# Seven products in place of eight for half of the first matrix product, in fp16, and three elementwise steps moved to GpSimd

## The chip, the cores and the metric

The kernel runs on one core of a Trainium2 chip. A core has five engines, each with a queue of its own that works in order: TensorE (matmuls, in the profile PE, with its weight loads PEld), VectorE (DVE), ScalarE (ACT), GpSimd (POOL) and SyncE (SP, which here only issues DMAs). Matmuls write to PSUM, which has eight banks of 512 fp32 values for each of 128 partitions; VectorE and ScalarE read and write it, GpSimd does not here. SBUF is the working memory. The metric is the time of one execution in microseconds (us), the median of several runs.

## The reference

Linear attention with phi(x) = elu(x) + 1, then a two-layer network with GELU on its output, for 8 batches of 8 heads, 576 rows and 64 values:

```python
def phi(x):
    return np.where(x > 0, x, np.exp(x) - 1.0) + 1.0
q_p, k_p = (phi(q), phi(k))
kv = np.einsum('bhsd,bhse->bhde', k_p, v)
z = np.sum(k_p, axis=2)
num = np.einsum('bhsd,bhde->bhse', q_p, kv)
den = np.einsum('bhsd,bhd->bhs', q_p, z)[..., None] + 1e-06
attn_out = num / den                                      # (8, 8, 576, 64)
x = attn_out.transpose(0, 2, 1, 3).reshape(B * S, H * D)  # 4608 x 512
h = x @ w_in                                              # w_in 512 x 2048
g = 0.5 * h * (1.0 + np.tanh(c * (h + 0.044715 * h * h * h)))
out = g @ w_out                                           # w_out 2048 x 512
```

Inputs and output are fp32.

## The kernel before

The 4608 rows of x are cut into nine groups. Groups 0 to 7 are the first 512 rows of each batch; group 8 gathers the last 64 rows of all eight. `iteration(j)` does group j's network, and beside it the attention of group j+1 and the preparation of later batches. Every engine issues in the order in which the Python code emits its instructions (`manual_schedule`), so the order is written by hand: a group's matmuls are a list of steps, and `at(j, slot, fn)` hangs other work behind step number `slot` of group j.

A group from 2 on has 16 steps for h and 7 for the output. A step `("h", m)` is four matmuls (`h_mm`, L394: 128 columns of `w_in_sb` as weights, 512 columns of the transposed x `xt` moving, both bf16, summed over d_model in one PSUM bank) and one GELU on ScalarE (`gelu`, L409) that writes block m of `g` in fp16. Its blocks are taken in the order 0, 8, 1, 9, ... The output of the group is then computed by Strassen's scheme in Winograd's form with seven products instead of eight (`Products`): g and w_out are each cut into two by two quarters, VectorE makes sums of quarters of g (`sums`, `third_sum`, `last_sum`, L763; those of w_out are made once, L752), each product is 16 matmuls of 256 columns (L790), and ScalarE and VectorE combine the results out of PSUM into `o_sb` (L834, L821, L862). Products come in the order 1, 5, 6, 7, 2, 4, 3.

The tiles of one PSUM pool share six banks ("b"), and a new tile takes the bank that came free first; the pair of banks "a" serves attention alone.

Attention of batch b is done in group b-1: after step 9 (group 2: 12) `nab_quads` issues 32 matmuls of q with the k-v products into four banks and the pair (L332), then 72 for the k-v product of batch b+1 (`kv_paired`, L254). At once VectorE divides (`divide`, L287 and L288) into `xs`, and SyncE issues four DMA transposes of `xs` into `xt` (L694). k and q go through `exp_of` (ScalarE), `linear_of` (max(x+1, 1), VectorE, L230) and `least_of` (their minimum, VectorE, L238); v is cast to bf16 by VectorE (L243); q is transposed by DMA (`least_q`, L671). For batches 5 to 7 this is `plan_prepare`: q's linear part and the v cast at the start of a group, k's linear part behind step 10, exponentials behind steps 15 and 16, minima behind 17 and 20. The loads of k, q and v (L94, L103) and of q's last rows (`load_rest`, L117; mapped in `plan_rest`) are issued by SyncE into a pool of seven buffers, `pld`. The output is stored by DMAs on ScalarE's queue (L875).

Of the kernel before, what the change touches and what calls it, by code (L numbers as in the profile page):

```python
# [8 lines left out]
FP32 = mybir.dt.float32  # L9
# [7 lines left out]
def kernel(  # L17
# [20 lines left out]
    P = 128  # L38
# [20 lines left out]
    pout = ctx.enter_context(tc.tile_pool(name="pout", bufs=2))  # L59
    psm = ctx.enter_context(tc.tile_pool(name="psm", bufs=2))  # L60
    pkv = ctx.enter_context(tc.tile_pool(name="pkv", bufs=1))
    ps_b = ctx.enter_context(
        tc.tile_pool(name="ps_b", bufs=6, space=bass.MemoryType.PSUM)
    )
# [6 lines left out]


    ident = const.tile([P, P + 64], BF16, name="ident")[:, 0:P]
    w_in_sb = const.tile([P, KM, d_ff], BF16, name="w_in_sb")
    w_out_sb = const.tile([P, 2, MM, N2], FP16, name="w_out_sb")
    w_sum = const.tile([P, 3, MM // 2, N2], FP16, name="w_sum")

    def bank(name, shape, dt=FP32):
        return ps_b.tile(shape, dt, name=name, tag="b")
# [98 lines left out]

    warm = const.tile([P, 512], BF16, name="warm")
    nc.vector.memset(warm, 0.0)  # L182
    make_identity(nc, ident)
    vps = [pkv.tile([P, J * NP, E], BF16, name=f"vp{i}") for i in range(2)]
    kvbds = [pkv.tile([P, NP, 2 * E], BF16, name=f"kvbd{b}") for b in range(3)]
    kvs = {b: pkv.tile([P, NP, E], BF16, name=f"kv{b}") for b in range(3, B)}
    for i in range(2):
        nc.gpsimd.memset(vps[i][:, :, D:E], 1.0)
# [32 lines left out]
            o, i = o[..., cs, :], i[..., cs, :]  # L221
        nc.scalar.activation(o, i, AF.Exp)  # L222

    def linear_of(name, b, hs=None):
        x = ld[name, b]
        hs = hs or slice(0, x.shape[1])
        if (name, b) not in phi:
            phi_tiles(name, b)
        o, i = maps_view(name, b, x, phi[name, b], hs)
        nc.vector.tensor_scalar(o, i, 1.0, 1.0, op0=ALU.add, op1=ALU.max)  # L230

    def least_of(name, b, hs=None, cs=None):
        p, e = phi[name, b], exps[name, b]
# [62 lines left out]

    def x_tile(b, c):
        if b not in xs:
            xs[b] = pxs.tile([P, C, d_model], BF16, name="xs")
        return xs[b][:, c]  # L300

    def by_parity(x):
# [12 lines left out]
            divide(by_parity(x)[:, a], ns[a].rearrange("p (u e) -> p u e", e=E))  # L315
        return x

    def nab_quads(qt_cs, bs, kv_b):

        ns = [[bank("n_ps", [P, 6 * E]) for _ in range(2)] for _ in range(2)]
        n_pair = pair_of_banks("n_ps")
        ns.append([n_pair[:, s] for s in range(2)])
        units = [(c, i, a) for c in range(C) for i in range(2) for a in range(2)]
        for n, (c, i, a) in enumerate(units):
            g = n // 6
            one = bs[c][0] == bs[c][1]
            for t in range(1 if one else 2):
                for s in range(2):  # L330
                    cs = slice(0, P) if one else slice(HP * t, HP * (t + 1))
                    nc.tensor.matmul(  # L332
                        ns[g][s][cs, E * (n - 6 * g) : E * (n - 6 * g + 1)],
                        lhsT=qt_cs[c][HP * s : HP * (s + 1), 2 * a + i, cs],
                        rhs=kv_of_head(bs[c][t], s, 2 * a + i),
                        skip_group_check=True,
                    )
        if kv_b is not None:
            for ii in range(2):
                kv_paired(kv_b, ii, lambda a, ii: n_pair[:, a, E * (4 + ii) : E * (5 + ii)])  # L340

        def x_of(transposed):
            x = pxs.tile([P, C, d_model], BF16, name="xs")
            x_v = x.rearrange("p c (i s a d) -> p s (c i) a d", s=2, a=2, d=D)
            for g in range(2):
                for s in range(2):
                    divide(
                        x_v[:, s, 3 * g : 3 * (g + 1)],
                        ns[g][s].rearrange("p (k a e) -> p k a e", a=2, e=E),
                    )  # L350
                for c in ((0,), (1, 2))[g]:
                    transposed(c, x[:, c])
            n_v = n_pair[:, :, 0 : 4 * E].rearrange("p s (k a e) -> p s k a e", a=2, e=E)
            divide(x_v[:, :, 6:8], n_v)
            transposed(3, x[:, 3])
            if kv_b is not None:
                nc.vector.tensor_copy(
                    out=kvs[kv_b].rearrange("p (a i) e -> p a i e", a=2),
                    in_=n_pair[:, :, 4 * E : 6 * E].rearrange("p a (i e) -> p a i e", e=E),
                )  # L360

        return x_of
# [19 lines left out]
        )  # L382

    def transpose_x(x, xt_c, fn, blocks=range(NP)):
        t_ps = bank("t_ps", [P, len(blocks), P], BF16)
        for n, i in enumerate(blocks):
            nc.tensor.transpose(t_ps[:, n, :], x[:, P * i : P * (i + 1)], ident)  # L387
        fn(out=xt_c[:, blocks.start : blocks.stop], in_=t_ps)

    xts, qts = {}, {}  # L390
# [35 lines left out]
    def first_batch():  # L426
# [44 lines left out]
        for i in range(2):  # L471
            cast_w_out(i, nc.gpsimd.tensor_copy)

        xts[0] = pt.tile([P, NP, MAIN], BF16, name="xt")
        x = {0: x_tile(0, 0)}

        def t(c, blocks=range(NP)):
# [34 lines left out]

    fill = {}

    def at(j, slot, fn, *args):


        fill.setdefault((j, slot), []).append((fn, args))  # L520
# [5 lines left out]
    def plan_second():  # L526
# [43 lines left out]

        def t(c):
            if c == 0:
                xts[b] = pt.tile([P, NP, MAIN], BF16, name="xt")
            transpose_x(x[c], xt_chunk(b, c), nc.scalar.copy)

        at(0, 15, maps)
# [38 lines left out]
    def plan_fourth():  # L615

        for slot, hs in zip((9, 13), halves):
            at(1, slot, linear_of, "k", 3, hs)
        at(1, 17, exp_of, "k", 3)
        at(1, 18, exp_of, "q", 3)  # L620
        at(1, 18, exp_of, "k", 4)
        at(1, 18, gelu_table)
        at(1, 20, least_of, "k", 3)
        at(1, 21, linear_of, "q", 3)
        at(2, 0, cast_v, 3)
        at(2, 0, least_q, 3)
        at(2, 4, kv_in_pair, 3)
        at(2, 5, linear_of, "k", 4)
        at(2, 5, least_of, "k", 4)
        at(2, 5, cast_v, 4)  # L630
        at(2, 8, linear_of, "q", 4)
        at(2, 15, exp_of, "q", 4)
        at(2, 16, exp_of, "k", 5)
        at(2, 19, least_q, 4)
        at(2, 22, linear_of, "k", 5)
        at(3, 0, least_of, "k", 5)

    def plan_prepare(j):

        b = j + 2  # L640
        has_k = b + 1 < B
        at(j, 0, linear_of, "q", b)
        at(j, 0, cast_v, b)
        at(j, 15, exp_of, "q", b)
        at(j, 17, least_q, b)
        if has_k:
            at(j, 10, linear_of, "k", b + 1)
            at(j, 16, exp_of, "k", b + 1)
            at(j, 20, least_of, "k", b + 1)

    def plan_rest(m):
        j = 5 + m // 2

        def least():
            least_of("qr", m)
            if m == 0:
                qts[B] = pt.tile([P, C, NP, P], BF16, name="qt")
            nc.sync.dma_start_transpose(
                out=qts[B][:, m], in_=phi["qr", m][:, 0].rearrange("p h d -> p (h d)")
            )  # L660

        at(j, 6 if j == 5 else 0, linear_of, "qr", m)
        at(j, 15, exp_of, "qr", m)
        at(j, 18, least)

# [24 lines left out]

    def transposed_x(b, c, x):
        if b not in xts:
            xts[b] = pt.tile([P, NP, MAIN], BF16, name="xt")
        nc.sync.dma_start_transpose(out=xt_chunk(b, c), in_=x)  # L694

    def plan_attention(b):


        def attention():
            bs = [(b, b) if b < B else (2 * c, 2 * c + 1) for c in range(C)]  # L700
            x_of = nab_quads([qts[b][:, c] for c in range(C)], bs, b + 1 if b + 1 < B else None)
            x_of(lambda c, x: transposed_x(b, c, x))

        at(b - 1, 12 if b == 3 else 9, attention)

    def evac(dst, src, on_scalar):
        (nc.scalar.copy if on_scalar else nc.vector.tensor_copy)(dst, src)
# [48 lines left out]
    class Products:  # L756
# [113 lines left out]
        def store(self, h, o_sb, fs=slice(0, d_model)):  # L870
# [5 lines left out]
            else:  # L876
                for t in range(2):
                    self.store_rest(2 * h + t, o_sb[:, t], fs)

    def iteration(j):  # L880
        xt = xts[j]
        if j < B:
            g = pg.tile([P, 2, MM, MAIN // 2], FP16, name="g")
        else:
            g = pg.tile([P, MM, 2, MAIN // 2], FP16, name="g").rearrange("p m a n -> p a m n")
        hs = [("h", m) for m in range(MM)]
        us = [range(m, m + 4) for m in range(0, MM, 4)]
        products = Products(j, g) if j else None
# [4 lines left out]
        elif j == 1:  # L893
# [6 lines left out]
            at(1, 14, products.sums, early)  # L900
            at(1, 17, products.sums, late)
            at(1, 19, products.last_sum)
        else:
            steps = [hs[i + n] for i in range(MM // 2) for n in (0, MM // 2)]
            steps += [("product", n) for n in (1, 5, 6, 7, 2, 4, 3)]
# [2 lines left out]
                at(j, slot, products.third_sum, ms)  # L908
            at(j, 16, products.last_sum)
        o_pss = {}  # L910
        for slot, step in enumerate(steps):
            if step[0] == "h":
                m = step[1]
                h_ps = h_begun.get(j, {}).get(m)
                if h_ps is None:
                    h_ps = bank("h_ps", [P, MAIN])
                    h_mm(h_ps, xt, m)
                gelu(j, g, m, h_ps)
            elif step[0] == "product":
                products.step(step[1])  # L920
            else:
# [3 lines left out]
                o_mm(o_pss[t], g, t, u, half=(j, slot - 0.5))  # L925
                if u.stop == MM:
                    finish(j, t, o_pss[t])
            run(j, slot)

    plan_second()  # L930
    plan_third()
# [15 lines left out]
        at(5, 1, load_rest, m + 2)  # L947
    for j in range(2, 7):
        at(j, 16, gelu_table)

    for j in range(B + 1):
        iteration(j)
# [30 lines left out]
```

## Time and profile before

| | |
|---|---|
| time, median of 3 runs (lowest to highest) | 271.81 us (271.79 to 272.06) |
| span of the profiled execution, first to last instruction | 270.2 us; the page gives no other time of that execution |
| TensorE's granted clock | 0.999 |
| busy: TensorE, its weight loads | 264.4 us, 170.8 us |
| busy: VectorE, ScalarE, GpSimd | 164.7 us, 166.0 us, 15.0 us |
| first matmul for h of groups 3 to 8 | 104.66, 132.11, 159.56, 187.01, 213.76, 240.60 us |

In a profile L394 is line 394 of the kernel; a row names engine, line, operation, and output<-inputs with their shapes. In brackets stands how long the engine had been idle before the instruction and who ended that. Matmuls overlap, so a row's own length is more than its pitch; the pitch is read from the starts or from the chain of work that ended last, which is followed back from the last instruction.

### The profile page before, as it was taken

The page shows a single profiled execution, that of the slowest core. Times are in us where ns is not written, and L with a number is a line of the kernel's source. Part 1 is how long each engine was busy: PE and PEld are TensorE (multiplying, and loading weights), DVE is VectorE, ACT ScalarE, POOL GpSimd, SP SyncE. Part 2 cuts the span into 40 slices and gives each one's busy share as a digit, 9 for nine tenths or more (in the row PEclk, how much of TensorE's full clock was granted, in tenths as well). Part 3 has the DMA queues.
Part 4 walks back from the last instruction along what each step waited for, and adds up shares of the span by engine and source line. Part 5 has one row for each costly group of instructions (what it writes and reads, how often), then busy time and mean ns, then how long its engine had stood idle before and what let it go on. Part 6 is the DMA issues. An engine that isn't in the chain of part 4 may idle for free.

```text
span 270.2 us, 5941 instructions
## 1 busy us (share of the span) xinstructions
PE 264.4 (98%) x2533; PEld 170.8 (63%) x2533; DVE 164.7 (61%) x265; ACT 166.0 (61%) x225; POOL 15.0 (6%) x21
## 2 busy tenths in 40 slices
PE   8999999999999999999999999999999999999994
PEld 2584456465854686558655874587458745874584
DVE  2860186988999966788738774693267326622262
ACT  4768877799776683668266926582665265028700
POOL 3056401000000000000000000000000000000000
PEclk9999999999999999999999999999999999999999
DMA  6999999995799998893699474219231412121004
GB/s 234 401 405 396 410 408 400 400 382 98 232 290 257 327 245 222 292 295 78 172 355 268 91 151 137 61 39 159 96 41 43 135 56 61 19 113 45 0 2 155
DMA packets 59786, 53.87 MB, mean 199 GB/s; under 512 B 35696, under 2 KB 45936, under 8 KB 59760
## 3 DMA queue, kind: packets, MB, share of 16 engines
q1 hardware_dynamic: 56880, 44.57, 58.4%
q10 hardware_dynamic: 2880, 8.91, 8.7%
q8 instruction: 20, 0.33, 0.5%
q14 instruction: 6, 0.05, 0.0%
HBM read 36.70 MB, written 9.44 MB: 171 GB/s over the span
## 4 chain that ended last, share of the span: by engine, by line
PE 92%; DMA 3%; DVE 2%; SPq 1%; issue 0%; ACT 0%
PE h_ps L394 45%; PE o_ps L790 36%; PE o_ps L734 5%; DMA v_x<-in_v_dram 3%; PE n_ps L332 1%; PE kv_ps L254 1%; PE n_ps L254 1%; PE n_ps L270 1%; PE t_ps L387 1%; SPq L94 1%; DVE s L763 0%; SPq L99 0%; PE t_ps L545 0%; DVE kvbd L686 0%; DVE vp L243 0%
## 5 line engine op out<-in xcount | busy, mean ns | idle before, releaser
L394 PE MATMUL h_ps<-xt,w_in_sb 128*128 128x512 bf16 (+1 forms) x628 | 128.4, 361 | 0.2 <-issue 0.2
L409 ACT ACTIVATE g<-h_ps 128x512 f16<-128x512 f32 x144 | 86.8, 616 | 59.5 <-PE h_ps L394 57.5
L394 PEld LDWEIGHTS <-w_in_sb 128*128 128x128 bf16 x628 | 58.2, 98 | 62.4
L790 PEld LDWEIGHTS <-g 128*128 128x128 f16 x624 | 60.9, 98 | 9.0 <-ACT g L409 0.2
L790 PE MATMUL o_ps<-w_out_sb,g 128*128 128x256 f16 x496 | 58.2, 273 | 0.0
L862 DVE TENSOR_TENSOR o_sb<-o_ps,o_sb 128x512 f32<-128x512 f32 (+1 forms) x42 | 27.9, 665 | 29.4 <-PE o_ps L790 28.5
L763 DVE TENSOR_TENSOR s<-g 128x1024 f16<-128x1024 f16 x18 | 12.4, 691 | 40.0 <-ACT g L409 39.9
L790 PE MATMUL o_ps<-w_sum,s 128*128 128x256 f16 x256 | 29.3, 273 | 0.0
L790 PEld LDWEIGHTS <-s 128*128 128x128 f16 x272 | 26.6, 98 | 3.1
L288 DVE TENSOR_TENSOR xs<-n_ps,r 128x384 bf16<-128x384 f32 (+2 forms) x44 | 25.6, 582 | 1.5
L222 ACT ACTIVATE k_e<-k_x 128x2304 bf16<-128x2304 f32 (+1 forms) x9 | 17.2, 1910 | 3.7 <-DVE k_p L238 2.9
L834 ACT COPY o_sb<-o_ps 128x512 f32<-128x512 f32 x8 | 4.7, 583 | 22.3 <-PE o_ps L790 22.3
L230 DVE TENSOR_SCALAR q_p<-q_x 128x2048 bf16<-128x2048 f32 (+1 forms) x9 | 9.9, 1101 | 13.2 <-DMA q_x<-in_q_dram 13.2
L222 ACT ACTIVATE q_e<-q_x 128x2048 bf16<-128x2048 f32 (+1 forms) x10 | 15.7, 1568 | 2.9 <-DMA q_x<-in_q_dram 2.9
L790 PE MATMUL o_ps<-w_sum,g 128*128 128x256 f16 x128 | 15.3, 273 | 0.0
L734 PE MATMUL o_ps<-w_out_sb,g 128*128 128x512 f16 x64 | 15.1, 379 | 0.0
L230 DVE TENSOR_SCALAR k_p<-k_x 128x2304 bf16<-128x2304 f32 (+1 forms) x10 | 11.1, 1113 | 4.2 <-DMA k_x<-in_k_dram 4.1
L422 ACT ACT_TABLE_LOAD x9 | 11.5, 1283 | 0.2
L431 PE MATMUL w_ps<-warm 128*128 128x512 bf16 x32 | 10.3, 484 | 1.2 <-DVE warm L182 1.2
L763 DVE TENSOR_TENSOR s<-s,g 128x1024 f16<-128x1024 f16 x16 | 11.1, 692 | 0.5
L238 DVE TENSOR_TENSOR k_p<-k_p,k_e 128x2304 bf16<-128x2304 bf16 (+1 forms) x9 | 11.0, 1221 | 0.7 <-ACT k_e L222 0.3
L243 DVE CAST vp<-v_x 128x2304 bf16<-128x2304 f32 (+1 forms) x9 | 11.0, 1225 | 0.5 <-DMA v_x<-in_v_dram 0.4
(63 smaller groups left out, 151.3 us busy)
## 6 DMA issues: line engine op xcount, KB each, us to landing
out_dram<-o_sb ACTq DMA_DIRECT2D x16, 512.0 KB, 3.9
k_x<-in_k_dram SPq DMA_DIRECT2D x7, 1152.0 KB, 9.3
v_x<-in_v_dram SPq DMA_DIRECT2D x7, 1152.0 KB, 12.0
q_x<-in_q_dram SPq DMA_DIRECT2D x6, 1024.0 KB, 12.6
w_st<-in_moe_w_in_dram SPq DMA_DIRECT2D x3, 1024.0 KB, 13.3
q_x<-in_q_dram SPq DMA_DIRECT2D x4, 512.0 KB, 8.7
w_st<-in_moe_w_out_dram SPq DMA_DIRECT2D x2, 1024.0 KB, 13.8
w_st<-in_moe_w_out_dram SPq DMA_DIRECT2D x4, 512.0 KB, 11.2
```

The costliest lines, as they stand in the source:

```text
L222: nc.scalar.activation(o, i, AF.Exp)
L230: nc.vector.tensor_scalar(o, i, 1.0, 1.0, op0=ALU.add, op1=ALU.max)
L238: nc.vector.tensor_tensor(p, p, e, op=ALU.min)
L243: fn(out=vp_paired(b)[:, :, us, 0:D].rearrange("p j u d -> p u j d"), in_=ld["v", b][:, us].rearrange("p u (j d) -> p u j d", d=D),)
L288: nc.vector.tensor_tensor(x_v, n_v[heads + (slice(0, D),)], r[heads + (None,)].to_broadcast(shape + [D]), op=ALU.mult,)
L394: nc.tensor.matmul(h_ps[:, ts], lhsT=w_in_sb[:, c, P * m : P * (m + 1)], rhs=xt[:, c, ts], start=(c == 0), stop=(c == KM - 1), skip_group_ ...
L409: nc.scalar.activation(g_v, h_v, AF.Gelu_apprx_tanh)
L422: nc.scalar.preload_act_table_set("gelu_apprx_tanh_and_others")
L734: nc.tensor.matmul(o_ps, lhsT=g[:, t // 2, m, P * (t % 2) : P * (t % 2 + 1)], rhs=w_out_sb[:, :, m, :], start=(m == 0), stop=(m == MM - 1),)
L763: nc.vector.tensor_tensor(out, i0, i1, op=op)
L790: nc.tensor.matmul(ps[t] if type(ps) is list else ps[:, t, :], lhsT=lhs[:, m, P * t : P * (t + 1)], rhs=rhs[:, m, :], start=(first and m = ...
L862: nc.vector.tensor_tensor(out, i0, i1, op=ALU.add)
```

## The change

In groups 3 to 8 eight of the sixteen h blocks (0, 1, 8, 9 and 4, 5, 12, 13) are no longer computed by `h_mm`. They form two units (`Quad`) of two by two quarters: 256 columns of f by 256 rows of x each, with d_model cut in two. A unit has seven products of four matmuls with 256 moving columns. Sums of quarters of w_in are made once, on GpSimd (`sum_w_in`, eight sums, hung behind step 1 of group 2), those of x once a group on VectorE (`sum_x`, four sums, behind step 21 of the group before). Products 1, 6, 5 and 3 follow each other in one bank, and what is in it is read between them: after product 1 by a copy into the bank of an earlier h block (the seed, onto which product 2 then adds), after 6 by a copy to SBUF (`u2`), after 5 by a sum with product 7's copy (`c22`), after 3 by GELU. Products 7 and 4 share another bank, to which VectorE adds `u2` in place. `QUAD_ORDER` puts the units' products between the eight plain blocks.

`w_in_sb`, `xs`, `xt` and the identity for x's transposes become fp16. In `plan_prepare` the v cast goes to GpSimd and two steps earlier, k's linear part to GpSimd, q's linear part to step 21 of the group before. Attention of batches 4 to 8 is issued behind slot 4 or 5 instead of 9, with the k-v matmuls of the next batch first, and its divides in three parts behind slots 5, 6 and 7. In groups 3 to 8 the sums of g all come behind slots 13 to 16. Two of the seven load buffers hold the sums and copies from group 2 on.

```diff
-    w_in_sb = const.tile([P, KM, d_ff], BF16, name="w_in_sb")
+    w_in_sb = const.tile([P, KM, d_ff], FP16, name="w_in_sb")
-    warm = const.tile([P, 512], BF16, name="warm")
+    warm = pg.tile([P, 512], BF16, name="warm", tag="g")
+    ident_x = pth.tile([P, P], FP16, name="ident_x")
+    t_sum = pth.tile([P, 3, KM // 2, MAIN // 2], FP16, name="t_sum")
+    make_identity(nc, ident_x)
-    def linear_of(name, b, hs=None):
+    def linear_of(name, b, hs=None, engine=nc.vector):
-        nc.vector.tensor_scalar(o, i, 1.0, 1.0, op0=ALU.add, op1=ALU.max)
+        engine.tensor_scalar(o, i, 1.0, 1.0, op0=ALU.add, op1=ALU.max)
...
+        order = list(enumerate(units))
+        if kv_first:
+            order = order[12:] + order[:12]
+            if kv_b is not None:
+                kv_into(kv_b, n_pair)
+            else:
+                order = order[4:10] + order[0:4] + order[10:]
+        for n, (c, i, a) in order:
...
+    FIRST = 3
-        at(2, 22, linear_of, "k", 5)
-        at(3, 0, least_of, "k", 5)
+        at(2, 15, linear_of, "k", 5, None, nc.gpsimd)
+        at(2, 20, least_of, "k", 5)
...
-        at(j, 0, linear_of, "q", b)
-        at(j, 0, cast_v, b)
+        at(j - 1, 21, linear_of, "q", b)
+        at(j - 1, 20, cast_v_paired, b, slice(0, NP), nc.gpsimd.tensor_copy)
-            at(j, 10, linear_of, "k", b + 1)
+            at(j, 2, linear_of, "k", b + 1, None, nc.gpsimd)
-        at(j, 6 if j == 5 else 0, linear_of, "qr", m)
+        at(j, 13, linear_of, "qr", m)
-        at(b - 1, 12 if b == 3 else 9, attention)
+        at(b - 1, 12 if b == FIRST else 4 if b + 1 < B else 5, attention)
+        for g, slot in enumerate((12, 12, 12) if b == FIRST else (5, 6, 7)):
+            at(b - 1, slot, part, g)
...
+    def begin_quads():
+        own["w"] = pld.tile([P, 9, KM // 2, 2 * P], FP16, name="w_quad", tag="ld")
+        own["r"] = pld.tile([P, 4, MAIN], FP32, name="rows", tag="ld")
+    def sum_w_in(u):
+        sums = ((s1, a21, a22, ALU.add), (s2, s1, a11, ALU.subtract))
+        sums += ((s3, a11, a21, ALU.subtract), (s4, a12, s2, ALU.subtract))
+        for out, i0, i1, op in sums:
+            nc.gpsimd.tensor_tensor(out, i0, i1, op=op)
+    def sum_x(j):
+        for out, i0, i1 in ((t3, b22, b12), (t1, b12, b11), (t2, b22, t1), (t4, b21, t2)):
+            nc.vector.tensor_tensor(out, i0, i1, op=ALU.subtract)
...
+            if name == 1:
+                self.b = bank("hq_ps", [P, 2, MAIN // 2])
+                self.product(self.b, a11, b11, True)
+                (nc.scalar.copy if self.j < B or self.u == 0 else nc.vector.tensor_copy)(seed, self.b)
+            elif name == 7:
+                self.w = bank("hq_ps", [P, 2, MAIN // 2])
+                self.product(self.w, s3, t3, True)
+                nc.vector.tensor_copy(m7, self.w)
+            elif name == 6:
+                self.product(self.b, s2, t2, False)
+                (nc.scalar.copy if self.j < B else nc.vector.tensor_copy)(u2, self.b)
+            elif name == 2:
+                self.product(seed, a12, b21, False)
+            elif name == "g11":
+                self.gelu(0, 0, seed)
+            elif name == 5:
+                self.product(self.b, s1, t1, False)
+                add(c22, self.b, m7)
+            elif name == 4:
+                self.product(self.w, a22, t4, False)
+            elif name == "a21":
+                add(self.w, self.w, u2)
+            elif name == 3:
+                self.product(self.b, s4, b22, False)
+                self.gelu(0, 1, self.b)
+            elif name == "g21":
+                self.gelu(1, 0, self.w)
+            elif name == "g22":
+                self.gelu(1, 1, c22)
...
+            at(j, 13, products.sums, early)
+            at(j, 14, products.sums, late)
+            at(j, 15, products.third_sum, slice(0, MM // 2))
+            at(j, 16, products.last_sum)
...
+    def QUAD_ORDER(plain, quad):
+        quad(0, (1,))
+        plain(2)
+        quad(0, (7, 2, 6, "g11"))
+        plain(10, 1)
+        quad(0, (5,))
+        plain(3, 4)
+        quad(0, (4,), 5)
+        quad(0, ("a21",), 6)
+        quad(0, ("g22", 3))
+        plain(11, 7)
+        quad(1, (1,))
+        quad(0, ("g21",), 8)
+        plain(6, 9)
+        quad(1, (7, 2, 6, "g11"), 11)
+        plain(14)
+        quad(1, (5, 4, "a21", "g22"))
+        plain(7, 13)
+        quad(1, (3,))
+        plain(15, 14)
+        quad(1, ("g21",), 15)
+    at(2, 0, begin_quads)
+    for u in range(NQ):
+        at(2, 1, sum_w_in, u)
+    for j in range(FIRST, B + 1):
+        at(j - 1, 21, sum_x, j)
```

The second argument of `plain` and the third of `quad` is the slot up to which hung work is emitted after that step.

## The prediction

> **What bounds the kernel now.** I read the page's shares first, then the chain in order of time, then the costliest groups, then the timeline of single stretches.
>
> ```profile
> PE 264.4 (98%) x2533; PEld 170.8 (63%) x2533; DVE 164.7 (61%) x265; ACT 166.0 (61%) x225; POOL 15.0 (6%) x21
> ...
> PE 92%; DMA 3%; DVE 2%; SPq 1%; issue 0%; ACT 0%
> ```
>
> TensorE is 92% of the chain that ended last; no other engine has more than two thirds of the span. So what counts is TensorE's own work and whoever makes it wait. The chain in order of time (start, length, what) shows one group, the fourth, whole, and above it the one stretch where VectorE is on the chain:
>
> ```profile
> 62.62 0.42 DVE kvbd L686
> 63.05 0.43 DVE kvbd L686
> 63.52 0.76 DVE k_p L230
> 64.28 0.61 DVE s L763
> 64.91 0.69 DVE s L763
> 65.88 0.70 DVE xs L288
> 66.72 0.40 PE n_ps L270 x4
> ...
> 132.27 8.63 PE h_ps L394 x40
> 140.91 0.60 PE n_ps L332 x32
> 141.51 0.71 PE n_ps L254 x72
> 142.21 5.29 PE h_ps L394 x24
> 147.50 12.23 PE o_ps L790 x112
> ```
>
> A group is 64 matmuls for h (13.92 us), attention (1.31) and 112 matmuls for the seven output products (12.23): 27.46 in all, nearly without holes. One h matmul of 512 columns costs 8.63/40 = 0.2158 us, one of 256 columns 12.23/112 = 0.1092. The timeline gives the hand-overs:
>
> ```profile
> 66.72 0.40 PE L270 MATMUL n_ps<-kvbd,qt 128*128 128x130 bf16 x4 [0.31 <-DVE xs L288]
> ...
> 102.23 6.18 SPq L671 DMA_TRANSPOSE qt<-q_p  x4
> ...
> 104.66 8.80 PE L394 MATMUL h_ps<-xt,w_in_sb 128*128 128x512 bf16 x40
> 105.78 0.60 ACT L409 ACTIVATE g<-h_ps 128x512 f16<-128x512 f32 x1 [3.83 <-PE h_ps L394]
> ...
> 120.71 0.69 DVE L763 TENSOR_TENSOR s<-g 128x1024 f16<-128x1024 f16 x1 [1.08 <-ACT g L409]
> 121.44 0.69 DVE L763 TENSOR_TENSOR s<-s,g 128x1024 f16<-128x1024 f16 x1
> 121.52 3.48 PEld L790 LDWEIGHTS <-s 128*128 128x128 f16 x32
> ```
>
> A block of h takes 4 x 0.2158 = 0.86, so the first ends at 105.52 and its GELU starts 0.26 later. After a product the reader starts 0.20 later (a product ends at 102.91, its sum starts at 103.11). From a reader's end to the waiting matmul it is 0.15 (the divide ends at 66.57, the matmul starts at 66.72). At 121.52 weights wait for s, 0.12 after VectorE's 0.69 us sum: this hand-over has no slack.
>
> **The change, part by part.**
>
> *TensorE's work.* Per group 32 matmuls of 512 columns go (6.91 us) and 56 of 256 columns come (6.12). Saved: 0.79, over six groups 4.74. fp16 costs nothing: loads of 128x128 weights take 98 ns in both types, a 512-column matmul 379 ns in both.
>
> *What a unit adds beside it.* ScalarE: two PSUM copies of 512 at 0.58 (row of o_sb L834), as many GELUs as before; 2.3 us per group against 57.5 us of waiting for h in all. VectorE: one copy and two sums of 512 out of PSUM at 0.69 each, 4.1 per group, and the four sums on x at about 0.38 (512-element sums of qr_p, 0.42 and less back to back), 1.5. It loses the v cast (1.36) and k's linear part (1.35): 2.9 more per group of 27. The totals fit; order decides. I walk group 4 with the numbers above, 0 being the end of the previous product 3:
>
> - The sums on x follow product 4's sum and q's map (1.22) and end at about 1.8; the first product that needs one starts at 1.30 and its sum is there at 0.7. No wait. Product 3's sum then ends at 2.5, the copy of product 7 at 3.2.
> - Product 6 ends at 2.61; its copy needs 0.20 + 0.58 + 0.15 = 0.93 before product 5, and block 10 between them covers 0.86: wait 0.07, in each unit.
> - Attention is now issued after block 3, at 4.84, and takes 1.39 with the gap of 0.09 seen before. Its fourth bank is block 3's, free at 5.70 + 0.15, and the k-v part and the first units run until 6.05: no wait.
> - VectorE divides from 6.25; each of the four takes 0.69, with the a21 sum after the second. Block 11 waits 0.04 for the first bank; products and block 6 get the second and the bank of product 3.
> - Part 2 and the kv copy keep VectorE until 11.0, so the second unit's copy of product 7 ends at 11.7 and product 4 (at 11.99) just does not wait.
> - h ends at 14.59 against 15.23 before. The s sums start after the last GELU (15.45) as before; product 5 waits 0.07.
>
> So group 4 gains 0.57. Group 3: its queries are transposed at 102.23 and after; the last of four starts at 106.5 and lands 2.4 to 4.5 later, 108.9 to 111.0, and attention wants them at 104.66 + 5.65 = 110.3: it may wait 0 to 0.7, I take 0.3, gain 0.3. Group 5: two maps of qr (0.42 each) stand before the s sums at slot 13 and delay product 5 by 0.28: gain 0.36. Groups 6 and 7 have no k-v part to cover the wait for the first divided bank (about 0.3) or block 3's GELU (0.08): h takes about 14.2 against 14.52 and 14.61; group 6 loses 0.27 more to qr: 0.05 and 0.36. Group 8 has GELUs of 0.74 in a permuted order, now partly two per step: its s sums come 0.4 late and eat the gain: 0.1. Sum: 0.3 + 0.57 + 0.36 + 0.05 + 0.36 + 0.1 = 1.7.
>
> *Moves that I cost at nothing.* Two of seven load buffers are kept: five are left; the next loads (86.82 to 88.00) go out behind four transposes on SP's queue that hold it until 86.72, and the buffers they need are free at 83.3; without the transposes the third would still wait only for the map of k. The x transposes are issued in three parts instead of one; SP holds them behind the loads of qr until 144.7 in group 4 and they land some 8 us before they are used. The output's store is issued on ScalarE's queue behind block 10's GELU; by then its sum (2.5) is done. The identity in fp16 is two short GpSimd instructions (0.20 and 0.29) before memsets that end 9 us before their reader; the warm tile in g's buffer is last read at 14.22, g is first written at 19.94.
>
> *GpSimd.* It gets eight sums for w_in (512 elements each), three v casts and three maps of k (2304). Its rows: a cast of 512 takes 0.61, of 2048 1.89, so 2304 some 2.1; two inputs or two operations bound these at once to twice that: the sums 4.9 to 9.8 us together, a map 2.1 to 4.3. The maps have about 10 us from the landing of k to their use. What they do to VectorE only one row shows:
>
> ```profile
> 14.58 1.04 POOL L140 CAST w_in_sb<-w_st 128x1024 bf16<-128x1024 f32 x1 [0.24 <-DMA w_st<-in_moe_w_in_dram]
> ...
> 18.40 0.69 DVE L140 CAST w_in_sb<-w_st 128x1024 bf16<-128x1024 f32 x1 [0.90 <-DMA w_st<-in_moe_w_in_dram]
> 18.43 1.56 POOL L140 CAST w_in_sb<-w_st 128x1024 bf16<-128x1024 f32 x1 [2.81 <-DMA w_st<-in_moe_w_in_dram]
> ```
>
> The same cast takes 0.52 longer beside a cast of VectorE that began first, and VectorE's is not longer. The other order occurs nowhere. Ends: VectorE never waits (0), or each VectorE instruction with SBUF operands that meets one waits it out. I take 0, as in the one row, for the sum. The Trainium skill, page "SBUF — State Buffer", section "Who interferes with whom", says that the pair of ports is locked by whichever starts first and that the other waits for the whole instruction; the row agrees in its one direction. By that rule VectorE would wait for the eight sums alone, by my estimate 1 to 3 us, and the total would be 271 to 273.
>
> *Sum.* The profiled execution spans 270.2; the median of the runs, 271.81, lies 1.6 above, which I take for what lies around the span. 270.2 - 1.7 = 268.5; with 1.6: **270.1**.
>
> **Rivals.**
>
> *GpSimd blocks VectorE (slower).* The eight sums depend only on a free buffer and w_in, so GpSimd does them long before the slot where they are written: any time after its last cast, 42.8. From 48.4 to 56 VectorE runs without a gap and the seventh product of group 1 waits for its end (56.32); from 62.6 to 66.7 it is on the chain itself. Three to five VectorE instructions each meeting a sum of 0.6 to 1.2 lose 2 to 5 us there. It decides from 1.7 on: 271.8 + 0.3 to + 3.3, say 273. Against it: the row above, and at 0.6 us per sum they may end before 48.4.
>
> *PSUM banks come in another order.* Of six banks one is held as a seed from one group to the next and attention takes four. If block 6 takes the third divided bank (9.1) instead of product 3's (8.1, wanted at 8.45), each group with attention loses 0.7: 5 x 0.7 = 3.5, total 273.6 at most, 272 if half. For it: the seeds leave two banks spare. Against: GELUs of before never hold up h.
>
> *The waits are shorter than walked.* With no wait at all the whole 4.74 comes: 267.1; with half of my waits 268.5.
>
> **How the numbers follow.** About 0.2%, 0.5 us, is what a measurement of this kernel can tell from no change. As walked, 269.0 to 271.2: 0.48. Shorter waits, 267.1 to 269.0: 0.14. GpSimd blocks: 0.26, mostly 271.5 to 274. Banks: 0.12, 271 to 273.5. Faster: nearly all of the first, the second, none of the third, little of the fourth: 0.61. Same (271.27 to 272.35): 0.13, from the last two. Slower: 0.26. The range leaves out half of the second case's low end and the top of the third: 267.8 to 273.6; the likeliest case's own is 269.0 to 271.2.
>
> **What would show it.** The chain's h part of group 4 should be 14.6 from the last output product to the first of the next, against 15.23, in groups 6 and 7 14.2, in 8 unchanged; all output products 12.23. Right: TensorE's holes in a group under 0.4, its h part with 32 matmuls of 512 and 56 of 256. GpSimd's eight sums in the timeline: where they lie and how long they take; VectorE instructions stretched or late beside them before 70 us, and a later start of group 3 than 104.66, would make the prediction wrong; so would a wait of block 6 or 11 of near 1 us for VectorE's divides, or a wait of attention in group 3 for queries.

## The result and the profile after

The changed kernel takes 286.2 us (median, 285.7 to 290.3) against 271.9 for the kernel before in the same set of runs: a ratio of 1.052, 95% interval 1.050 to 1.054. It is slower by 14.3 us; 270.1 was predicted, and the range ended at 273.6. One of its four runs, that of 290.3 us, was a slow one (granted clock 0.964, the others 0.976 to 0.981) and counts in the median but not in the ratio. The profiled execution took 286.4 us, 284.3 of them its span.

First the page of the changed kernel: busy time of the engines, the granted clock in 40 slices, and the chain of work that ended last, by engine.

```profile
PE 265.5 (93%) x2677; PEld 186.2 (65%) x2677; DVE 210.3 (74%) x316; ACT 172.1 (61%) x254; POOL 62.0 (22%) x37
...
PEclk9999999999999779999599999999999999999999
...
PE 79%; DVE 15%; DMA 3%; issue 1%; SPq 1%; ACT 0%; DVEq 0%
```

TensorE's share of the chain fell from 92% to 79% and VectorE's rose from 2% to 15%: some 37 us more of the path are VectorE's. The granted clock, at full speed throughout before, drops in three slices. The chain in order of time (start, length, what) shows where.

```profile
82.13 1.85 DVE k_p L234
...
88.42 1.57 DVE s L792
...
99.14 3.75 DVE s L792
102.94 11.88 PE o_ps L819 x92
...
128.07 6.03 DVE s L792
134.12 3.24 DVE s L792 x2
137.41 11.87 PE o_ps L819 x92
...
190.86 12.23 PE o_ps L819 x112
```

Two stretches, 82 to 103 and 127 to 137, are VectorE's, with sums of 0.69 us that take 1.6 to 6; after each, 92 products take 11.9 us where 112 take 12.23 elsewhere (0.129 us each, against 0.109). From group 5 on TensorE runs without holes. Its timeline shows the four long ones before that (in brackets how long it had stood still, and who ended that):

```profile
95.94 1.43 PE L410 MATMUL h_ps<-xt,w_in_sb 128*128 128x512 f16 x4 [4.28 <-DVE xs L292]
102.94 4.90 PE L819 MATMUL o_ps<-w_sum,s 128*128 128x256 f16 x28 [2.10 <-DVE s L792]
134.14 1.04 PE L819 MATMUL o_ps<-w_sum,s 128*128 128x256 f16 x4 [3.12 <-DVE s L792]
137.41 4.88 PE L819 MATMUL o_ps<-w_sum,s 128*128 128x256 f16 x28 [2.23 <-DVE s L792]
```

The timeline of GpSimd (start, length, line, operation, and in brackets the idle time before it) lies over these stretches; its third map, in group 4, lies mostly beside VectorE work out of PSUM.

```profile
79.60 1.92 POOL L929 TENSOR_TENSOR w_quad<-w_in_sb 128x512 f16<-128x512 f16 x1 [36.85 <-DVE vp L247]
...
94.07 8.93 POOL L234 TENSOR_SCALAR k_p<-k_x 128x2304 bf16<-128x2304 f32 x1
102.97 2.63 POOL L247 CAST vp<-v_x 128x2304 bf16<-128x2304 f32 x1
126.25 7.96 POOL L234 TENSOR_SCALAR k_p<-k_x 128x2304 bf16<-128x2304 f32 x1 [20.64 <-PE h_ps L410]
134.17 2.64 POOL L247 CAST vp<-v_x 128x2304 bf16<-128x2304 f32 x1
155.92 7.96 POOL L234 TENSOR_SCALAR k_p<-k_x 128x2304 bf16<-128x2304 f32 x1 [19.11 <-PE hq_ps L955]
```

And VectorE's timeline beside the second map:

```profile
126.77 0.69 DVE L986 TENSOR_TENSOR rows<-hq_ps,rows 128x512 f32<-128x512 f32 x1 [0.76 <-PE hq_ps L955]
127.38 0.69 DVE L986 TENSOR_TENSOR hq_ps<-hq_ps,rows 128x512 f32<-128x512 f32 x1
127.98 6.11 DVE L792 TENSOR_TENSOR s<-g 128x1024 f16<-128x1024 f16 x1
134.12 0.69 DVE L792 TENSOR_TENSOR s<-s,g 128x1024 f16<-128x1024 f16 x1
134.73 2.62 DVE L792 TENSOR_TENSOR s<-g 128x1024 f16<-128x1024 f16 x1
```

The map runs from 126.25 to 134.21. Two VectorE instructions that begin inside it and have an input in PSUM take 0.69 us, as ever. The first one with both inputs in SBUF, an s sum of 0.69 us, starts at 127.98 and ends at 134.09, with the map. One more gets through at 134.12; the third meets the v cast, which runs from 134.17 to 136.81, and ends half a us behind it, at 137.35. This is the rival "GpSimd blocks VectorE", with other instructions than it named.

The groups, from the end of one group's output products to the next, in us (from the chains of both kernels; the last column is the fastest version found below):

| group | before | after | predicted gain | fastest version |
|---|---|---|---|---|
| 3 begins at | 104.82 | 114.82 | | 105.22 |
| 3 | 27.45 | 34.45 | 0.3 | 26.68 |
| 4 | 27.46 | 27.16 | 0.57 | 26.66 |
| 5 | 27.45 | 26.66 | 0.36 | 26.66 |
| 6 | 26.74 | 26.15 | 0.05 | 26.15 |
| 7 | 26.84 | 26.19 | 0.36 | 26.19 |
| 8 | 26.05 | 25.49 | 0.1 | 25.49 |

So the loss lies in groups 2 and 3 alone, 10.0 and 7.0 us. Groups 4 to 8 are all faster, by 0.30 to 0.79.

### The profile page after: what moved, and what is told of

It is laid out like the page before. It is cut to its first block, busy times and chain, and to the rows that moved or that the text cites. A ratio compares the mean times of both kernels' runs of the same rounds, so it can differ in the third digit from the quotient of the medians.

```text
span 284.3 us, 6359 instructions
## 1 busy us (share of the span) xinstructions
PE 265.5 (93%) x2677; PEld 186.2 (65%) x2677; DVE 210.3 (74%) x316; ACT 172.1 (61%) x254; POOL 62.0 (22%) x37
## 4 chain that ended last, share of the span: by engine, by line
PE 79%; DVE 15%; DMA 3%; issue 1%; SPq 1%; ACT 0%; DVEq 0%
PE o_ps L819 33%; PE h_ps L410 24%; PE hq_ps L955 11%; DVE s L792 7%; PE o_ps L763 5%; DMA v_x<-in_v_dram 3%; PE h_ps L955 2%; DVE xs L292 1%; PE n_ps L347 1%; PE kv_ps L258 1%; DVE vp L247 1%; DVE k_p L234 1%; PE n_ps L274 1%; PE n_ps L258 1%; DVE k_p L242 1%
## 5 line engine op out<-in xcount | busy, mean ns | idle before, releaser
L410 PE MATMUL h_ps<-xt,w_in_sb 128*128 128x512 f16 (+2 forms) x436 | 93.6, 355 | 4.5 <-DVE xs L292 4.3
L425 ACT ACTIVATE g<-h_ps 128x512 f16<-128x512 f32 x96 | 57.0, 613 | 23.2 <-PE h_ps L410 22.9
L819 PEld LDWEIGHTS <-g 128*128 128x128 f16 x624 | 61.6, 99 | 10.2 <-issue 0.5
L410 PEld LDWEIGHTS <-w_in_sb 128*128 128x128 f16 x436 | 39.6, 98 | 36.8 <-DVE xs L292 5.3
L234 POOL TENSOR_SCALAR k_p<-k_x 128x2304 bf16<-128x2304 f32 x3 | 24.9, 8285 | 39.8 <-PE h_ps L410 20.6
L292 DVE TENSOR_TENSOR xs<-n_ps,r 128x384 f16<-128x384 f32 (+2 forms) x44 | 25.6, 582 | 1.5
L792 DVE TENSOR_TENSOR s<-g 128x1024 f16<-128x1024 f16 x18 | 24.5, 1358 | 1.4 <-ACT g L425 1.3
L955 PEld LDWEIGHTS <-w_quad 128*128 128x128 f16 x192 | 18.6, 98 | 8.9 <-issue 0.5
L955 PE MATMUL hq_ps<-t_sum,w_quad 128*128 128x256 f16 x144 | 21.6, 272 | 0.0
L986 DVE TENSOR_TENSOR rows<-hq_ps,rows 128x512 f32<-128x512 f32 x12 | 8.3, 692 | 11.8 <-PE hq_ps L955 11.8
L955 PEld LDWEIGHTS <-w_in_sb 128*128 128x128 f16 x144 | 13.8, 98 | 3.6
L929 POOL TENSOR_TENSOR w_quad<-w_in_sb 128x512 f16<-128x512 f16 x4 | 8.0, 2012 | 36.8 <-DVE vp L247 36.8
```

The costliest lines, as they stand in the source:

```text
L234: engine.tensor_scalar(o, i, 1.0, 1.0, op0=ALU.add, op1=ALU.max)
L292: nc.vector.tensor_tensor(x_v, n_v[heads + (slice(0, D),)], r[heads + (None,)].to_broadcast(shape + [D]), op=ALU.mult,)
L410: nc.tensor.matmul(h_ps[:, ts], lhsT=w_in_sb[:, c, P * m : P * (m + 1)], rhs=xt[:, c, ts], start=(c == 0), stop=(c == KM - 1), skip_group_ ...
L425: nc.scalar.activation(g_v, h_v, AF.Gelu_apprx_tanh)
L792: nc.vector.tensor_tensor(out, i0, i1, op=op)
L819: nc.tensor.matmul(ps[t] if type(ps) is list else ps[:, t, :], lhsT=lhs[:, m, P * t : P * (t + 1)], rhs=rhs[:, m, :], start=(first and m = ...
```

## The experiments

Theory A: a GpSimd instruction on SBUF holds up every VectorE instruction whose operands are all in SBUF, to its own end; the products in place of h blocks do TensorE good. Theory B: the units of seven products hold TensorE up themselves, through their chain of copies and sums. All runs are variants of the changed kernel unless it says otherwise, and each is compared with the kernel before on the same chip (271.8 to 272.0 in each set).

### K's maps back on VectorE

```diff
-        at(2, 15, linear_of, "k", 5, None, nc.gpsimd)
+        at(2, 17, linear_of, "k", 5)
-            at(j, 2, linear_of, "k", b + 1, None, nc.gpsimd)
+            at(j, 10, linear_of, "k", b + 1)
```

> k's three linear maps go back to VectorE; v's casts and the eight w_in sums stay on GpSimd. Theory A (a GpSimd instruction on SBUF shuts VectorE's SBUF-only instructions out until it ends; the long maps do most of the harm): the two s sums that took 3.82 and 6.11 us in groups 2 and 3 fall back under 1 us, group 3's period from 34.45 to about 26.9, group 2 gives back 3.1 + 1.9 us and perhaps 1.8 of the lower clock; the eight sums still cost group 2 about 4 us. 286.2 - 7.6 - 5.1 (to 6.9) - 0.4 = 271.3 to 273.1. Theory B (the seven-product units hold TensorE up by their own chain): above 282.

Measured: 276.4 us, 9.8 less than the change; ratio to before 1.016 (1.015 to 1.018). Theory B falls. It is 3 us above theory A's upper end: the eight sums cost more than the 4 us I had left them.

### Nothing new on GpSimd

```diff
 (with the edit above)
-        at(j - 1, 20, cast_v_paired, b, slice(0, NP), nc.gpsimd.tensor_copy)
+        at(j - 1, 20, cast_v, b)
-            nc.gpsimd.tensor_tensor(out, i0, i1, op=op)
+            nc.vector.tensor_tensor(out, i0, i1, op=op)
-    for u in range(NQ):
-        at(2, 1, sum_w_in, u)
+    at(2, 17, sum_w_in, 0)
+    at(3, 3, sum_w_in, 1)
```

> Nothing new is left on GpSimd: k's maps, v's casts and the w_in sums are all on VectorE, the sums behind group 2's products and in group 3. Theory A: group 3 starts at about 105, groups 3 to 8 take 0.3 to 0.8 us less each than before, as groups 4 to 8 already did with the change; 271.8 - 3.5 = 268.3, up to 269.5 if VectorE's 4 more us per group are felt. Theory B: above 280.

Measured: 269.5 us, ratio 0.991 (0.989 to 0.992): the upper end. The change without its GpSimd part is faster than the kernel before, although VectorE has more to do. What is left to gain is in group 3 (28.2 us): TensorE waits 1.1 us there for a sum on x, which stands behind 25 us of VectorE work without a gap.

### The GpSimd part alone, in the kernel before

```diff
 (kernel before)
+    def linear_of(name, b, hs=None, engine=nc.vector):
-        at(2, 22, linear_of, "k", 5)
-        at(3, 0, least_of, "k", 5)
+        at(2, 15, linear_of, "k", 5, None, nc.gpsimd)
+        at(2, 20, least_of, "k", 5)
-        at(j, 0, cast_v, b)
+        at(j - 1, 20, cast_v_paired, b, slice(0, NP), nc.gpsimd.tensor_copy)
-            at(j, 10, linear_of, "k", b + 1)
+            at(j, 2, linear_of, "k", b + 1, None, nc.gpsimd)
```

> The kernel before, bf16 and without any seven-product units on h, with only k's three maps and the v casts of batches 5 to 7 moved to GpSimd, at the slots of the change. Theory A: VectorE's s sums wait for maps of 8 us in up to four groups, 4 to 7 us each; 280 to 292. Theory B: no difference, 271.5 to 273.

Measured: 282.2 us, ratio 1.037 (1.034 to 1.039), 10.2 us slower without one product of the new kind. The timeline of this run, GpSimd's line and VectorE's beside it:

```profile
93.66 8.30 POOL L230 TENSOR_SCALAR k_p<-k_x 128x2304 bf16<-128x2304 f32 x1 [50.38 <-DMA k_x<-in_k_dram]
...
93.45 0.69 DVE L763 TENSOR_TENSOR s<-g 128x1024 f16<-128x1024 f16 x1
94.18 7.66 DVE L763 TENSOR_TENSOR s<-s,g 128x1024 f16<-128x1024 f16 x1
```

The s sum that was under way when the map came took its 0.69; the map took 0.34 longer than its 7.96; the next sum waited for the map's end. Whoever begins first is not disturbed here, in both directions.

### K's maps on GpSimd in four pieces

```diff
-        at(2, 15, linear_of, "k", 5, None, nc.gpsimd)
+        for n in range(4):
+            at(2, 15, linear_of, "k", 5, slice(n, n + 1), nc.gpsimd)
 (and the same for the maps of batches 6 and 7)
```

> Each of k's maps on GpSimd is cut into four instructions of 576 elements, about 2 us each. If whoever has begun holds the port to the end of its instruction and VectorE is let in between two pieces: an s sum waits 2.0 us at most (3.82 and 6.11 us with whole maps), but the next one may meet the next piece; 278 to 284. If the map slows VectorE by its traffic and not by whole instructions: s sums as long as before, 286.

Measured: 274.7 us, ratio 1.010 (1.009 to 1.012), below the range given: 11.5 of the 14.3 us come back though GpSimd does the same work. The timeline, in the stretch where the whole map had cost 3.1 us:

```profile
94.05 10.65 POOL L234 TENSOR_SCALAR k_p<-k_x 128x576 bf16<-128x576 f32 x4
...
99.03 0.68 DVE L794 TENSOR_TENSOR s<-g 128x1024 f16<-128x1024 f16 x1
99.75 1.03 DVE L794 TENSOR_TENSOR s<-s,g 128x1024 f16<-128x1024 f16 x1
100.70 0.68 DVE L794 TENSOR_TENSOR g<-g 128x1024 f16<-128x1024 f16 x1
```

VectorE hardly waits here; GpSimd does (10.65 us for four pieces, 8.47 where it takes least). So the length of one instruction is the price, not the traffic. But VectorE does not only come in between two pieces, as I had expected. In group 4 of this run an s sum with both inputs in SBUF lies wholly inside the record of one piece, and neither is stretched:

```profile
149.65 2.13 POOL L234 TENSOR_SCALAR k_p<-k_x 128x576 bf16<-128x576 f32 x1
150.51 0.68 DVE L794 TENSOR_TENSOR s<-g 128x1024 f16<-128x1024 f16 x1
```

So a piece of 576 elements does not shut VectorE out to its own end, as theory A has it for every GpSimd instruction; why pieces and whole maps differ is open. It was not tried how far smaller pieces would carry.

### Only the eight sums on GpSimd, early and late

First k's maps and v's casts on VectorE, the sums as in the change:

> k's maps and v's casts on VectorE; only the eight w_in sums stay on GpSimd. Against the run with k's maps alone on VectorE (276.4): there one s sum of group 2 took 2.56 us beside a v cast, and one g sum of group 3 2.94. If the casts cost what those lines show (1.9 and up to 1.7, the second mostly off the path): 273.5 to 275. If the casts cost nothing on the path: 276 to 276.5. What is left above 269.5 is then the price of the eight sums.

Measured: 275.5 us (274.5 to 276.3), ratio 1.013 (1.011 to 1.015). That is 0.9 less than with the casts on GpSimd too, and how much of it is the casts' is open: in the two profiles the clock is low for 3.3 and for 7 us behind the same hole of TensorE in group 2, which alone can make such a difference.

Then the same with a one-element copy on GpSimd ahead of each four sums, which reads something that VectorE writes late:

```diff
+    def sum_w_in_behind(u, late):
+        nc.gpsimd.tensor_copy(own["w"][:, 4 * u, 0, 0:1], late())
+        sum_w_in(u)
-    for u in range(NQ):
-        at(2, 1, sum_w_in, u)
+    at(2, 9, sum_w_in_behind, 0, lambda: phi["q", 4][:, 0, 0, 0:1])
+    at(2, 22, sum_w_in_behind, 1, lambda: own["w"][:, 8, 0, 0:1])
```

> As the run with only the eight w_in sums on GpSimd (275.5), but the sums begin later: a one-element GpSimd copy ahead of each four reads something that VectorE writes late (q's map of batch 4 at 88, the last sum on x at 108), so the sums lie where VectorE works out of PSUM (divides, copies, a21 sums). Theory A, only VectorE instructions with SBUF alone are shut out: the first four run from 89 to 93.7 and hold one s sum up by 0.7 at most, the others from 108 to 113 hold nothing; group 3 takes 26.7 where it took 28.4 with the sums on VectorE: 269.5 - 1.0 to 1.8 = 267.7 to 268.5. Rival, GpSimd's sums cost wherever they lie: 273 to 275.

Measured: 269.4 us, ratio 0.991 (0.989 to 0.993). Nothing but the moment of eight instructions was moved, and 6.1 us went. The timeline of GpSimd and VectorE:

```profile
90.92 1.15 POOL L929 TENSOR_TENSOR w_quad<-w_quad,w_in_sb 128x512 f16<-128x512 f16 x1
...
91.43 0.56 DVE L292 TENSOR_TENSOR xs<-n_ps,r 128x384 f16<-128x384 f32 x1
```

Beside divides out of PSUM neither side is stretched: a sum takes 1.15 us, where among SBUF instructions it took up to 2.27. The total missed its range by 0.9. The first s sum of group 2 meets the fourth w_in sum and takes 1.64, 0.95 more than its 0.69, and the wait for a sum on x stayed (0.8 us in group 3). With the w_in sums on VectorE that wait was 1.1, so most of it was not their doing.

### What a map costs on GpSimd, by form

```diff
 (on the four pieces; output without gaps)
+            if n == 1:
+                engine.tensor_scalar(o, i, 1.0, None, op0=ALU.max)
+            if n == 2:
+                engine.tensor_copy(o, i)
```

> The price of k's map on GpSimd, by form. Each of the four pieces of 576 elements is written without a gap in its output (other order of the values, so k's map is wrong); the second piece has max alone and no addition, the third is a plain cast. Whole maps of 2304 took 7.96 us, so a piece some 2.0. If the price goes by operation: max alone 1.0 to 1.1, cast 0.5 to 0.6. If it goes by the form of the instruction: max alone 2.0. If the gaps in the output were the price: the first and fourth piece clearly under 2.0. Total 270 to 275.

Measured: 274.3 us in one run. The timeline, pieces 1 to 3 in a stretch where VectorE reads PSUM:

```profile
144.16 2.13 POOL L244 TENSOR_SCALAR k_p<-k_x 128x576 bf16<-128x576 f32 x1 [10.62 <-DVE r L301]
146.27 1.65 POOL L239 TENSOR_SCALAR k_p<-k_x 128x576 bf16<-128x576 f32 x1
147.87 0.66 POOL L242 CAST k_p<-k_x 128x576 bf16<-128x576 f32 x1
```

The gaps in the output are not the price (2.13 without, 8.47/4 = 2.12 with them). Nor is it the number of operations alone: max alone takes 1.65, three quarters of both. A tensor_scalar takes 2.9 to 3.7 ns an element on GpSimd, a cast 1.1.

### Versions meant to be fast

Sums and k's maps on VectorE, v's casts on ScalarE, q's map a slot later:

> A version meant to be the fastest: k's maps on VectorE, v's casts on ScalarE behind the copy of product 2, all eight w_in sums on VectorE behind group 2's products, q's map one slot later than the sums on x. With everything on VectorE group 3 took 28.4 us against 26.65 in group 4, 1.1 of it one wait for a sum on x. If that goes: 269.5 - 1.1 to 1.8 = 267.7 to 268.4. If ScalarE's casts (some 2.1 us each, the length of k's exp of the same size) hold up the copies and GELUs: 269.5 or more.

Measured: 270.6 us, ratio 0.995 (0.994 to 0.996): slower than with everything on VectorE. The casts cost nothing, groups 4 to 8 are as there. But all eight sums now stand ahead of the minimum for q of batch 4, so its queries are transposed late. An output sum of group 2 stands behind them too, and TensorE waits 0.73 us for it. The chain in group 3:

```profile
103.64 1.14 SPq L688
...
107.91 4.67 DMA qt<-q_p
112.62 0.67 PE n_ps L347 x32
```

TensorE waits 1.75 us for the queries: the hand-over that the prediction named for group 3, brought on here by another edit.

K's maps in pieces and v's casts on GpSimd, sums on VectorE, q's map a slot later:

> k's maps on GpSimd in four pieces, v's casts on GpSimd, w_in's sums on VectorE behind group 2's products. Theory A: the cut maps let VectorE in between, and nothing else of the change costs: 274.7 less what the sums cost there (about 7 us, group 2 with the lower clock): 267.5 to 269. If the pieces still cost 1 us per group: 270 to 272.

Measured: 274.4 us, but twelve runs lay between 270.2 and 277.95, so it is inconclusive. The profiled run (a span of 273.9) shows the same wait, longer, and what follows it on TensorE:

```profile
113.99 1.06 PE L347 MATMUL n_ps<-kv,qt 64*128 64x65 bf16 x32 [2.86 <-DMA qt<-q_p]
...
116.67 1.91 PE L410 MATMUL h_ps<-xt,w_in_sb 128*128 128x512 f16 x4
```

After the hole of 2.86 us everything takes up to twice its time until 120 (1.91 us for four matmuls whose row is 1.03 elsewhere), at a granted clock of 0.50. That the spread comes from runs with and without this hole would fit, but is only argued.

The sums late on GpSimd, v's casts on ScalarE, k's maps on VectorE, q's map a slot later:

> The same with v's casts on ScalarE and q's map a slot later: VectorE has 1.36 us less per group in groups 2 to 4. 267.4 to 268.3 if VectorE was still felt in group 3; no difference to the run beside it (within 0.3) if not. If q's later map makes the queries' transposes late for attention: up to 269.5.

Measured: 268.7 us, ratio 0.989 (0.987 to 0.990). Last, k's maps of batches 6 and 7 behind the s sums:

```diff
-            at(j, 10, linear_of, "k", b + 1)
+            at(j, 17, linear_of, "k", b + 1)
```

> As the fastest run so far (268.7), with k's maps of batches 6 and 7 on VectorE behind the s sums instead of between the copy of product 7 and its sum. There one product waited 0.42 us for that sum, which stood behind a map that began only when k had landed (116.39). Theory: group 3 loses 0.4 less: 268.2 to 268.5. If the map behind the s sums makes the next group's sums on x late: 268.7 to 270.

Measured: 268.0 us, ratio 0.986 (0.984 to 0.987): faster than both kernels, with no hole of TensorE over 0.2 us from group 3 on.

The change's own division of work, with the maps in pieces and the sums late:

> The change's own division of the work, all three kinds on GpSimd, with two edits: k's maps in four pieces, and the eight w_in sums made to begin late. Theory A (length and moment of GpSimd's instructions are the whole loss): 274.7 less the 6.1 that moving the sums was worth: 268.5 to 270. If GpSimd's work as such costs (16 pieces and casts beside VectorE): 271.5 to 274.

Measured: 275.6 us, ratio 1.012 (1.010 to 1.014), against both theories as I had worded them. The timeline of VectorE and TensorE:

```profile
104.51 3.27 DVE L242 TENSOR_TENSOR k_p<-k_p,k_e 128x2304 bf16<-128x2304 bf16 x1 [2.03 <-POOL k_p L234]
...
109.99 1.01 PE L961 MATMUL hq_ps<-t_sum,w_quad 128*128 128x256 f16 x4 [3.55 <-ACT g L425]
```

The cut map of batch 5, behind the late sums, ends at 104.48. VectorE's minimum for k, next in its queue, waits 2.03 for it and then, beside the v cast, takes 3.27 instead of 1.35. Queued behind it are q's map and the sums on x, and for these TensorE stands still for 3.55 us (the bracket names a GELU of ScalarE, which ended at 109.98; but in the run with nothing new on GpSimd the same product began 0.06 before that GELU's end, so it is the first sum on x, which ends at about 109.85, that it waits for). Then come 6 us at a clock of 0.50, worth 3 more: 6.5 together, the difference to 269.4 being 6.2. Length and moment of GpSimd's instructions are not all; its results also come late to an engine that takes its work in order.

## Why the prediction was wrong, by its steps

- **"GpSimd ... I take 0, as in the one row, for the sum": this is the step that failed.** The one row had VectorE first, so it could not show what happens in the other order, and the trace of before had no GpSimd work beside VectorE's s sums at all. In place of 0, VectorE's sums of 0.69 us take 3.8 and 6.1 beside the maps. From the change to the run with late sums and both maps and casts on VectorE it is 286.2 - 269.4 = 16.8 us: 9.8 for the maps, 0.9 with the casts, 6.1 for the moment of the sums. TensorE's holes in the trace of the changed kernel for s and xs are 7.5 + 4.3 = 11.8; its matmuls at the lower clock lose some 5 (92 products twice 1.8, 16 products 1.3, one block 0.4).
- **The sizes under it.** "A map 2.1 to 4.3" was worked from casts: a map took 7.96, almost twice the upper end. The sums were bounded well (4.9 to 9.8; 9.2 for eight at 1.15).
- **The place.** The rival put the sums "any time after 42.8". Their buffer was free only when VectorE had cast v of batch 3, and they began at 79.60, where VectorE has a long row of SBUF work (from 82 to 95, stretched). The rival's mechanism was right, and its price of 2 to 5 us less than a third; it had been given a chance of 0.26. The maps, which cost most, were in none of its instructions. The sign named for it came: the first matmul of group 3 starts at 114.66 instead of 104.66.
- **"The maps have about 10 us from the landing of k to their use."** This looked at who needs the map, not at who needs VectorE while it runs. The second map lay over the s sums of group 3, which took 7.0 longer than before, the v cast behind the map included. The third, in group 4, lay mostly over divides: it stretched one s sum to 1.35 and the v cast behind it another to 2.59, and the group took 27.16 where the fastest version takes 26.66.
- **TensorE's work was right.** 0.79 us saved per group: group 5 gives exactly that. h blocks in fp16 cost as much as before, and output products take 12.23 in undisturbed groups.
- **The walk was too dark.** It left 1.7 us of 4.74. The fastest version gains 0.77, 0.80, 0.79, 0.59, 0.65 and 0.56 in groups 3 to 8, 4.16 in all. The waits of 0.28 for the maps of qr and the late sums in group 8 did not come: the output products take 12.23 and 12.24 there. Of the wait for a divided bank in groups 6 and 7 some 0.2 us came: in group 6 of the fastest version block 11 would be due at 191.39 by the pitch of the products and starts at 191.59, just after the first divide has ended at 191.54. H took 13.92 in group 6, with 14.2 walked. The rival "waits are shorter" was right on this term, the rival "banks" wrong: no group loses its 0.7 us.
- **Sums on x "No wait".** True from group 4 on. In group 3 it holds only while VectorE isn't full behind group 2: 1.1 us with all the work on VectorE.
- **Two load buffers fewer.** Right for the loads' issue; but k of batch 6 landed at 116.39 in one run, and a map placed ahead of it in VectorE's queue held a product up by 0.42.

The Trainium skill, page "SBUF — State Buffer", section "Who interferes with whom", would have given the mechanism: whichever starts first holds the shared ports for its whole instruction; a VectorE instruction with two SBUF inputs meets a GpSimd instruction that reads SBUF, and one with at most one SBUF input outside the two-port modes does not. The runs with whole maps agree, with 0.56 to 0.69 us for instructions that read PSUM and 6.11 and 7.66 for s sums of 0.69. The pieces do not agree with "for its whole instruction": the sum of 0.68 us inside a piece was not held up. I cited the rule and went by the row; where a row shows only one order of two events, it can't speak against a rule for the other order. And "VectorE would wait for the eight sums alone" did not follow from the rule: maps and casts on GpSimd read SBUF as well, and the s sums met both.

## What to carry to other kernels

Work moved to GpSimd is not free because GpSimd is idle: ask which VectorE instructions with all operands in SBUF start while it runs, and who waits for those. Lay long GpSimd instructions beside VectorE work out of PSUM (a one-element copy that reads a late result is enough to time them) or cut them, and look at what is queued behind the first reader of their result. Price an operation on GpSimd by a row of the same form; a cast says nothing of a tensor_scalar.

## What the runs showed of the hardware

- Holes in TensorE's work of 2.86, 3.12, 3.55, 4.28 and 5.18 us each led to 3 to 7 us at a granted clock of 0.50 (with 2.86 and 3.55, 113.1 to 119.9 and 109.2 to 116.0, from just before the end of the hole), which adds 1.5 to 3 us to the price of the hole. Holes of 1.75 and 1.86 us did not; one of 2.10 us, five us behind one of 4.28, did. The Trainium skill, page "TensorE: Matmul & The Clock Gate", Part 1, has a window of about 3.4 us for going idle; here holes of 2.86 and 3.12 us were enough.
- A tensor_scalar of two operations from fp32 to bf16 takes 3.5 to 3.7 ns an element on GpSimd, 7.96 us for 2304, against 1.35 us on VectorE; with one operation 2.9 ns, and a cast 0.9 to 1.1.
- Beside the pieces of a cut map VectorE's sums took 0.68 to 1.03 us in the stretch shown, two of them inside the record of one piece (99.22 to 101.70), and the four pieces took 10.65 us in place of 8.47.
